# An attention stage re-ordered by a second search, with short operations moved between VectorE, ScalarE and GpSimd

## The chip, the core and the metric

The kernel runs on one core of a Trainium2 chip. The metric is the device time of one execution in microseconds (us); the median of three timed runs stands for a version. The trace names the engines PE (TensorE's matrix multiplications), PEld (its weight loads), DVE (VectorE), ACT (ScalarE), POOL (GpSimd) and SP (SyncE, which issues most DMAs).

## What is computed

A two-step attention feeds a mixture of experts with a greedy assignment of tokens:

```python
def sm_attn(qq, kk, vv):
    s = scale * np.matmul(qq, kk.transpose(0, 1, 3, 2))
    s = s - np.max(s, axis=-1, keepdims=True)
    a = np.exp(s)
    a = a / (np.sum(a, axis=-1, keepdims=True) + 1e-09)
    return np.matmul(a, vv)
p_packed = sm_attn(p, k, v)              # 32 packed rows per head
out = sm_attn(q, p_packed, p_packed)     # 8 batches, 8 heads, 576 tokens, 64 wide
...
logits = x @ w_gate                      # x: 4608 tokens x 512, 8 experts
# tokens go to experts in falling order of logit, at most 576 to an expert
h = np.maximum(x[mask] @ w1[e], 0.0)
out[mask] = h @ w2[e]
```

## The kernel before

The work has three parts. **Attention** goes through 16 groups, each of one batch and four heads. **The router** finds, expert by expert, the threshold that gives each expert its 576 tokens. **The experts** run eight times: gather the tokens, two matrix products in split fp32 (three products for one), scatter.

The attention of one group g is a chain of named steps. DMAs `ld_k`, `ld_q`, `ld_v`; `t_k` and `t_q` turn k and q on VectorE (L353, L354); `s1` on TensorE (L368), `max1` (L380), `exp1`, `rec1` on GpSimd (L391), `tr1` (L400), `a_cp`, `mm_pp` (L416, L418) give the packed rows, `pp_ev` scales them, `pp_t` turns them (L433), `pp_hi` and `pp_lo` (L441) split them in a rounded part and a rest. Then `s2` (L368 again), and the second softmax in a turned layout: `t_s` (L470, L472), `max2` (L476), `sub2` (L481), `exp2` (L485), `sum2` (L491 as one reduction on VectorE, or L497 and L499 as a tree of six additions on GpSimd), `rec2` (L503), `nrm2` (L508), `t_a` (L512), `th` (L516) and `tl` (L521). Five products `x0` to `x4` (L543) follow, whose results `xe0` to `xe4` copy out of PSUM on ScalarE (L553) or on VectorE (L551); `x_st` stores them and `x_lg` adds up the router's logits (`xl0` to `xl4` on VectorE, L566 and L568, for the last two groups).

The order of these steps on each engine is found by a planner, `attention_plan`. It holds a table of steps with engine, length and inputs, and a set of waits for buffers; a list scheduler goes through them in time and takes, on each engine, the ready step with the lowest number in `PRIO` (three columns: groups 0 and 1, groups 2 to 12, groups 13 to 15). `OTHER` names the steps, by group, that go to their second engine, VectorE instead of GpSimd or ScalarE, with the lengths in `on_dve`. Numbers from 44 on stand for halves, since groups 14 and 15 do their second softmax in two halves: 44 and 45 are the halves of group 14, 46 and 47 those of group 15. A step with its group is written sub2.12 below, and with a or b for a half. `early` and `late` are VectorE steps of the router that the planner places too: its constants, and the first look at the logits of all but the last group.

Behind attention, `limit_t` to `limit_c` derive the range of thresholds, `build_a` to `build_v` the values to count, `steps(0, 2)` makes two rounds of counting, `found` draws up the list of expert 0's tokens and starts the loads of its weights by a number `ei` that `expert` computes (L964), and `fl` (L1264) tells whether two rounds were enough. From there to the end the experts follow, in an order that a second planner sets.

Of the kernel before, what the change touches and what calls it, by code (L numbers as in the profile page):

```python
# [15 lines left out]
OP = mybir.AluOpType  # L16
AX = mybir.AxisListType
# [33 lines left out]
    'ld_q': (44.062, 1020.3516, -400.897), 'ld_v': (93.4338, 230.7431, 3.103), 't_k': (-303.2684, 1053.8496, 1263.3541),  # L51
    's1': (-344.5301, 1030.018, 1343.4823), 'max1': (-1141.7006, 595.7444, 1747.411), 'exp1': (1482.9927, 300.9519, 957.0636),
    'rec1': (-364.306, -478.1404, -1528.0943), 'rec1b': (469.6087, -649.4928, 805.8052), 'tr1': (-544.6934, 406.9933, 869.3049),
    'a_cp': (-42.2238, -980.4241, -316.4565), 'mm_pp': (-314.1418, 269.0578, -274.3437), 'pp_ev': (161.5907, -716.4717, 357.7413),
# [128 lines left out]
def attention_plan(fn, on_pool, early, late, groups=16):  # L183
# [3 lines left out]
        ('t_k', 'DVE', 1.46, ['ld_k']), ('s1', 'PE', 1.93, ['t_k']), ('max1', 'DVE', .68, ['s1']),  # L187
        ('exp1', 'ACT', 1.0, ['max1']), ('rec1', 'Pool', .17, ['exp1']), ('rec1b', 'DVE', .08, ['rec1']),
        ('tr1', 'PE', .6, ['exp1']), ('a_cp', 'ACT', .66, ['tr1']), ('mm_pp', 'PE', .9, ['a_cp', 'ld_v']),
        ('pp_ev', 'ACT', 1.28, ['mm_pp', 'rec1b']), ('pp_t', 'DVE', .37, ['pp_ev']), ('t_q', 'DVE', 1.46, ['ld_q']),  # L190
        ('s2', 'PE', 2.12, ['pp_t', 't_q']), ('pp_hi', 'ACT', .41, ['pp_ev']), ('pp_lo', 'Pool', .7, ['pp_hi']),
        ('wg_hi', 'ACT', .31, ['s2', 'pp_hi']), ('wg_lo', 'Pool', .17, ['wg_hi', 'pp_lo']),
        ('t_s', 'DVE', .8, ['s2']), ('max2', 'DVE', .64, ['t_s']), ('sub2', 'Pool', 1.12, ['max2']),
# [1388 lines left out]
```

## Time and profile before

| what | value |
|---|---|
| median of 3 runs | 637.77 us (637.51 to 638.63) |
| profiled execution | 643.15 us, span 641.4 us |
| PE busy | 594.6 us, 93% of the span |
| PEld busy | 496.7 us, 77% |
| DVE busy | 412.9 us, 64% |
| ACT busy | 336.1 us, 52% |
| POOL busy | 368.5 us, 57% |
| mean granted TensorE clock | 0.986 |

The busy shares are means over parts with different limits: attention takes the first 148 us or so, the router's first rounds go to 166 us, and the experts hold the rest. The profiled execution is 5.4 us above the median of the runs.

### The profile page before, as it was taken

What the parts mean: (1) busy time and instruction counts of PE and PEld (TensorE: products, weight loads), DVE (VectorE), ACT (ScalarE), POOL (GpSimd) and SP (SyncE); (2) the same over time, 40 slices, a digit from 0 to 9 for tenths busy, and PEclk for the clock granted to TensorE, in tenths of its full rate; (3) what the DMA queues carried; (4) which work ended last, traced back from release to release, by engine and by line L of the source; (5) the groups of instructions that cost most, each with busy time, mean ns of one, the idle gap of its engine ahead of it and who ended that gap; (6) DMA issues with size and microseconds to landing.
All of it is one profiled execution on the core that took longest, in us unless ns stands there. A gap on an engine that the chain in (4) does not pass through costs nothing. (4 is left out here: it accounts for less than half of the span.)

```text
span 641.4 us, 12439 instructions
## 1 busy us (share of the span) xinstructions
PE 594.6 (93%) x4099; PEld 496.7 (77%) x4101; DVE 412.9 (64%) x1508; ACT 336.1 (52%) x853; POOL 368.5 (57%) x592
## 2 busy tenths in 40 slices
PE   6999899983699999999899999998999999999996
PEld 3678677752388888888788788797888989889984
DVE  7899999997666767657557966964792144162111
ACT  5677777762383774764664565385334235233102
POOL 8378676680570793962954783675447756725003
PEclk9899999997999999999999999999999999999998
DMA  8999996332820634432566365438333864812002
GB/s 274 369 341 309 296 319 198 111 112 75 269 68 6 226 107 150 155 108 76 196 231 155 132 214 116 141 137 245 103 100 107 261 157 144 241 44 75 1 1 78
DMA packets 76953, 103.42 MB, mean 161 GB/s; under 512 B 11792, under 2 KB 57104, under 8 KB 76880
## 3 DMA queue, kind: packets, MB, share of 16 engines
q1 hardware_dynamic: 70464, 83.64, 41.2%
q0 software_dynamic: 5888, 18.88, 8.5%
q8 instruction: 35, 0.57, 0.4%
q14 instruction: 38, 0.31, 0.2%
q10 hardware_dynamic: 528, 0.02, 0.1%
HBM read 77.74 MB, written 24.77 MB: 160 GB/s over the span
## 5 line engine op out<-in xcount | busy, mean ns | idle before, releaser
L1159 DVE SCALAR_TENSOR_TENSOR h<-hp,h 128x288 fp32r<-128x288 f32 (+2 forms) x192 | 59.5, 351 | 116.3 <-ACT h L1154 111.8
L1135 POOL TENSOR_TENSOR w2l<-w2s,w2h 128x256 fp32r<-128x256 f32 x124 | 92.0, 773 | 68.6 <-ACT w2h L1129 68.5
L1135 POOL TENSOR_TENSOR w1l<-w1s,w1h 128x256 fp32r<-128x256 f32 x124 | 91.1, 767 | 58.2 <-ACT w1h L1129 51.6
L1168 PE MATMUL y<-w2h,h 128*128 128x512 f32 x256 | 104.5, 408 | 0.0
L1170 PE MATMUL y<-w2h,h 128*128 128x512 f32 x256 | 101.0, 395 | 0.0
L1169 PE MATMUL y<-w2l,h 128*128 128x512 f32 x256 | 101.0, 395 | 0.0
L1148 PE MATMUL hp<-xh,w1h 128*128 128x288 f32 x512 | 91.5, 301 | 4.6 <-DVE h L1159 1.7
L1148 PE MATMUL hp<-xl,w1h 128*128 128x288 f32 x512 | 90.6, 299 | 0.6 <-DVE xl L1111 0.3
L1154 ACT ACTIVATE h<-hp 128x288 fp32r<-128x288 f32 x128 | 48.7, 406 | 80.4 <-issue 37.4
L1148 PE MATMUL hp<-xh,w1l 128*128 128x288 f32 x512 | 90.4, 298 | 0.0
L1148 PEld LDWEIGHTS hp<-xh,w1h 128*128 128x128 f32 x512 | 77.1, 188 | 10.8 <-DVE h L1159 1.7
L868 ACT ACTIVATE ja<-Vt,nT 128x288 bf16<-128x288 f32 x118 | 63.2, 536 | 36.7 <-DVE nT L894 34.5
L1148 PEld LDWEIGHTS hp<-xl,w1h 128*128 128x128 f32 x512 | 74.9, 188 | 1.3 <-DVE xl L1111 0.5
L1201 POOL DMA_INDIRECT out_dram<-xg,gi x40 | 39.1, 979 | 63.7 <-DVE fl L1427 36.9
L1148 PEld LDWEIGHTS hp<-xh,w1l 128*128 128x128 f32 x512 | 74.6, 188 | 0.1
L1129 ACT CAST w1h<-w1s 128x1024 fp32r<-128x1024 f32 x32 | 33.5, 1047 | 56.2 <-DMA w1s<-in_moe_w_dram 17.8
L1067 POOL DMA_INDIRECT xg<-xd,gi x40 | 39.0, 975 | 32.4 <-DVE Lw L989 21.7
L1170 PEld LDWEIGHTS y<-w2h,h 128*128 128x128 f32 x256 | 48.0, 187 | 11.5
L1169 PEld LDWEIGHTS y<-w2l,h 128*128 128x128 f32 x256 | 48.1, 188 | 8.2
L1168 PEld LDWEIGHTS y<-w2h,h 128*128 128x128 f32 x256 | 48.0, 188 | 8.3
L1129 ACT CAST w2h<-w2s 128x1024 fp32r<-128x1024 f32 x32 | 33.5, 1048 | 32.4 <-issue 13.3
L543 PE MATMUL xp<-P,th 128*128 128x264 f32 (+1 forms) x154 | 37.1, 329 | 7.0 <-ACT xs L553 4.5
(269 smaller groups left out, 1146.1 us busy)
## 6 DMA issues: line engine op xcount, KB each, us to landing
w1s<-in_moe_w_dram SPq DMA_DIRECT2D x32, 512.0 KB, 6.0
w2s<-in_moe_w_dram SPq DMA_DIRECT2D x32, 512.0 KB, 4.3
kl<-in_k_dram SPq DMA_DIRECT2D x16, 576.0 KB, 5.4
ql<-in_q_dram SPq DMA_DIRECT2D x16, 576.0 KB, 6.2
vl<-in_v_dram SPq DMA_DIRECT2D x32, 256.0 KB, 5.2
xd<-xs SPq DMA_DIRECT2D x32, 256.0 KB, 3.3
xg<-xs SPq DMA_DIRECT2D x20, 288.0 KB, 6.3
xs<-xg SPq DMA_DIRECT2D x20, 256.0 KB, 3.8
```

Of the source, the lines that this page charges most:

```text
L543: nc.tensor.matmul(xp[:m, :264], T[a, g][:, o:o + m], T[w, g], start=i == 0, stop=i == 2)
L868: nc.scalar.activation(ja, Vf, AF.Sign, bias=S_['nT'][:, j:j + 1], scale=-1.0, accum_out=cp[:, j:j + 1])
L1067: nc.gpsimd.indirect_dma_start(out=X['xg', k, c][:m], out_offset=None, in_=xd, in_offset=bass.IndirectOffsetOnAxis(ap=X['gi', k][:m, c:c + ...
L1129: nc.scalar.copy(X[n + 'h', k, q], X[n + 's', k, q])
L1135: eng.tensor_sub(X[n + 'l', k, q][r], X[n + 's', k, q][r], X[n + 'h', k, q][r].bitcast(F32))
L1148: nc.tensor.matmul(X['hp', k, f, n], X[W, k, q][:, d, 128 * r:128 * r + 128], X[Z, k][:, d, 288 * n:288 * n + 288], start=i + d == 0, stop ...
L1154: nc.scalar.activation(X['h', k, f][:, 288 * n:288 * n + 288], X['hp', k, f, n], AF.Relu)
L1159: V.scalar_tensor_tensor(h[:, o:o + b - a], p[:, a - 288 * n:b - 288 * n], 0.0, h[:, a:b].bitcast(F32), op0=OP.max, op1=OP.subtract)
L1168: nc.tensor.matmul(y, hh, wh, start=f == 0, stop=False)
L1169: nc.tensor.matmul(y, hh, wl, start=False, stop=False)
L1170: nc.tensor.matmul(y, hl, wh, start=False, stop=f == 7)
L1201: s = nc.gpsimd.indirect_dma_start(out=out, out_offset=bass.IndirectOffsetOnAxis(ap=X['gi', k][:m, t:t + 1], axis=0), in_=X['yo', k, t][:m ...
```

## The change

`PRIO` holds new numbers throughout, and `OTHER` other steps, so that steps of attention change places on all engines and some change their engine. The planner's table gets other lengths (of 29 rows and 6 entries of `on_dve`), `wg_hi` now waits for `t_s`, and two dependences are added. `bf` is taken from the logits directly on the first round, without `best` and an addition. `limit_b`'s product, `expert(0)` and `fl` go from VectorE to GpSimd, `limit_c`'s copy to ScalarE, and the second `build_t` stands ahead of the first `build_v`.

```diff
-    'p_ld_0': (-908.3844, 0.0, 0.0), 'p_t_0': (-275.3561, 0.0, 0.0), 'p_b0_0': (-1206.1704, 0.0, 0.0),
+    'p_ld_0': (-2253.0361, 0.0, 0.0), 'p_t_0': (21.1347, 0.0, 0.0), 'p_b0_0': (-815.0743, 0.0, 0.0),
...
-    'xe2': (0,), 'xe0': (1, 3, 4, 5, 6, 7, 11, 13,), 'xe4': (1, 4, 8, 11,), 'sum2': (2, 3, 5, 9, 10, 11, 13, 44, 45, 46, 47,),
-    'sub2': (3, 11, 12, 13, 44,), 'xe1': (3, 6, 7, 8, 9, 11,), 'pp_lo': (5, 7,), 'nrm2': (5, 11, 45,), 'tl': (6, 44, 45,),
-    'xe3': (8, 11, 15,), 'pp_ev': (14,),}
+    'sum2': (1, 3, 6, 11, 12, 13, 44, 45, 46, 47,), 'xe0': (1, 10, 12,), 'xe4': (1, 2, 6, 8, 9, 15,),
+    'xe1': (3, 6, 8, 10, 12, 13, 14,), 'xe2': (3, 7, 10, 13,), 'nrm2': (4, 44, 46,), 'tl': (6, 8,), 'pp_lo': (7,),
+    'xe3': (9, 11, 13,), 'sub2': (13,),}
...
-    on_dve = {'pp_ev': .72, 'pp_lo': .48, 'sub2': .68, 'sum2': .55, 'nrm2': .8, 'tl': .7}
+    on_dve = {'pp_ev': .76, 'pp_lo': 1.6, 'sub2': 1.1, 'sum2': .64, 'nrm2': .8, 'tl': 1.2}
...
+            P.dep((f'xl{c}', g), (f'xe{c}', g))
+    for g in range(1, groups):
+        P.dep(('x_lg', g - 1), ('x_lg', g))
...
-        V.tensor_scalar(bm[:, :4], C['lim'][:1], bm[:, 4:], None, op0=OP.mult)
+        nc.gpsimd.tensor_scalar(bm[:, :4], C['lim'][:1], bm[:, 4:], None, op0=OP.mult)
...
-        V.tensor_copy(st0, S_['pm'][:, :4])
+        nc.scalar.copy(st0, S_['pm'][:, :4])
...
+    def build_f(a, b):
+        V.reduce_max(bf[:, a:b], L0[:, a:b], axis=AX.X)
...
-    build_a(L0, 31, 36)
+    build_f(31, 36)
+    build_e(L0, 31, 36)
     limit_b()
     build_b(L0, 31, 36)
+    build_t(1, 2)
     build_v(0, 1)
-    build_t(1, 2)
...
-        expert(0)
+        expert(0, nc.gpsimd)
...
-    V.tensor_scalar(fl, mk, 1.0, None, op0=OP.is_ge)
+    nc.gpsimd.tensor_scalar(fl, mk, 1.0, None, op0=OP.is_ge)
```

On VectorE the first large move is in the middle of attention. Before, between `max2.5` and `max1.8`, stand `rec2.4`, `pp_t.6` and the subtraction `pp_lo.5` (L441):

```order
L476 TENSOR_REDUCE mx<-sb 128x18
L503 RECIPROCAL sm<-sm 128x18
L433 STREAM_TRANSPOSE PT<-pf_156 128x4x2x32
L441 TENSOR_TENSOR P_1084<-pf_158,P_1069 128x256
L380 TENSOR_REDUCE st<-s_1056 128x1
```

With the change the same place holds `rec2.4`, `max2.5`, the product `nrm2.4` (L512 is the former L508), `pp_t.6`, `t_a.4` and a copy `xe1.3`:

```order
L507 RECIPROCAL sm<-sm 128x18
L480 TENSOR_REDUCE mx<-sb 128x18
L512 TENSOR_TENSOR e_169<-e_169,sm 128x18x32
L437 STREAM_TRANSPOSE PT<-pf_156 128x4x2x32
L516 STREAM_TRANSPOSE at<-e_169 128x576
L555 COPY xs<-xp 128x264
```

`pp_lo.5` has gone to GpSimd, and `nrm2.4` has come from there.

On GpSimd, before, `pp_lo.10` (L441) is followed by `tl.8` (L521), `sub2.9` (L481), `wg_lo.10`, `sub2.10`, `nrm2.9` (L508), `rec1.13` and `pp_lo.11`, and there is no sum:

```order
L441 TENSOR_TENSOR P_1674<-pf_157,P_1662 128x256
L521 TENSOR_TENSOR tl<-at,th 128x576
L481 TENSOR_TENSOR sb<-sb,mx 128x576
L452 TENSOR_TENSOR P_1674<-wf,P_1662 128x8
L481 TENSOR_TENSOR sb<-sb,mx 128x576
L508 TENSOR_TENSOR e_168<-e_168,sm 128x18x32
L391 TENSOR_SCALAR st<-st 128x1
L441 TENSOR_TENSOR P_1818<-pf_158,P_1811 128x256
```

With the change `pp_lo.10` is followed by `sub2.10`, `nrm2.9`, `wg_lo.10` and the tree of `sum2.10` (L501 and L503); the tree of `sum2.9` stands a few rows ahead:

```order
L445 TENSOR_TENSOR P_1720<-pf_157,P_1701 128x256
L485 TENSOR_TENSOR sb<-sb,mx 128x576
L512 TENSOR_TENSOR e_168<-e_168,sm 128x18x32
L456 TENSOR_TENSOR P_1720<-wf,P_1701 128x8
L501 TENSOR_TENSOR su<-e_169 128x18x16
L501 TENSOR_TENSOR su<-su 128x18x8
L501 TENSOR_TENSOR su<-su 128x18x4
L501 TENSOR_TENSOR su<-su 128x18x2
L501 TENSOR_TENSOR su<-su 128x18
L503 TENSOR_TENSOR sm<-su,e_169 128x18
L395 TENSOR_SCALAR st<-st 128x1
```

`sum2.9` and `sum2.10` were reductions on VectorE; on GpSimd each is six additions in a row. `tl.8` has gone to VectorE.

Behind attention, on VectorE, the flag and the number of the expert stood between the test (L934) and the assignment (L955, L956):

```order
L933 SCALAR_TENSOR_TENSOR key<-pcv,act_79 128x8
L934 TENSOR_REDUCE mk<-key 128x1
L1264 TENSOR_SCALAR fl<-mk 128x1
L964 TENSOR_SCALAR ei<-mk 128x1
L955 SCALAR_TENSOR_TENSOR m_2468<-bf,Tf,kk 128x36
```

With the change they are on GpSimd, behind the last `tl` halves and `limit_b`'s product:

```order
L525 TENSOR_TENSOR tl<-at,th 128x256
L525 TENSOR_TENSOR tl<-at,th 128x320
L817 TENSOR_SCALAR bmax<-lim,bmax 1x4
L1276 TENSOR_SCALAR fl<-mk 128x1
L975 TENSOR_SCALAR ei<-mk 128x1
L1280 TENSOR_LOAD fl
```

On VectorE the assignment now follows the test directly. From the list of expert 0's tokens on, all engines have the same instructions in the same order as before.

## Rows read from the trace of the kernel before

**Rows 1.** Busy time by stretch: us, then busy (and instructions) of each engine, clock, DMA
```profile
43.59:85.97 42.38, 40.25 (x408) 31.49 (x397) 42.22 (x89) 31.88 (x99) 31.27 (x56) 1.00 0.93 297
85.97:121.86 35.89, 35.21 (x334) 27.07 (x332) 34.78 (x80) 26.83 (x83) 24.18 (x40) 1.00 0.67 217
134.92:148.21 13.29, 9.61 (x54) 7.07 (x54) 12.49 (x43) 9.27 (x28) 7.79 (x16) 1.00 0.41 135
176.66:641.40 464.74, 447.50 (x2795) 390.19 (x2795) 255.29 (x1078) 223.76 (x526) 254.16 (x358) 1.00 0.42 130
```

**Rows 2.** Single lines on DVE: count, shortest/median/longest ns, first and last start
```profile
L441 DVE TENSOR_TENSOR P<-pf,P x2: 956/1878/2801, 61.1 to 82.0; 128x256 fp32r<-128x256 f32 x2
L481 DVE TENSOR_TENSOR sb<-sb,mx x5: 702/1278/1455, 46.5 to 133.5; 128x576 f32<-128x576 f32 x4, 128x256 f32<-128x256 f32 x1
L508 DVE TENSOR_TENSOR e<-e,sm x3: 740/759/953, 71.2 to 137.5; 128x576 f32<-128x576 f32 x2, 128x320 f32<-128x320 f32 x1
L521 DVE TENSOR_TENSOR tl<-at,th x3: 422/691/1580, 79.8 to 141.0; 128x576 fp32r<-128x576 f32 x1, 128x256 fp32r<-128x256 f32 x1, 128x320 fp32r<-128x320 f32 x1
L491 DVE TENSOR_REDUCE sm<-e x11: 409/722/772, 45.0 to 139.9; 128x18 f32<-128x594 f32 x7, 128x8 f32<-128x264 f32 x2, 128x10 f32<-128x330 f32 x2
L551 DVE COPY xs<-xp x21: 370/392/435, 40.5 to 138.8; 128x264 f32<-128x264 f32 x17, 64x264 f32<-64x264 f32 x4
L829 DVE TENSOR_TENSOR bf<-best,tkn x8: 164/196/841, 143.6 to 400.9; 128x36 f32<-128x36 f32 x6, 128x31 f32<-128x31 f32 x1, 128x5 f32<-128x5 f32 x1
```

**Rows 3.** Timeline around pp_lo.5: start us, length us, instruction
```profile
61.09 2.80 DVE L441 TENSOR_TENSOR P<-pf,P 128x256 fp32r<-128x256 f32 x1
...
61.29 1.15 POOL L508 TENSOR_TENSOR e<-e,sm 128x576 f32<-128x576 f32 x1
62.40 1.15 POOL L481 TENSOR_TENSOR sb<-sb,mx 128x576 f32<-128x576 f32 x1
```

**Rows 4.** Single lines on POOL, and the first and last addition of one sum tree
```profile
L441 POOL TENSOR_TENSOR P<-pf,P x14: 723/736/1287, 18.9 to 138.7; 128x256 fp32r<-128x256 f32 x14
L481 POOL TENSOR_TENSOR sb<-sb,mx x13: 617/1160/1165, 27.0 to 136.8; 128x576 f32<-128x576 f32 x10, 128x320 f32<-128x320 f32 x2, 128x256 f32<-128x256 f32 x1
L508 POOL TENSOR_TENSOR e<-e,sm x15: 617/1157/1676, 32.7 to 141.2; 128x576 f32<-128x576 f32 x12, 128x256 f32<-128x256 f32 x2, 128x320 f32<-128x320 f32 x1
L521 POOL TENSOR_TENSOR tl<-at,th x15: 730/1417/1730, 36.2 to 143.5; 128x576 fp32r<-128x576 f32 x13, 128x256 fp32r<-128x256 f32 x1, 128x320 fp32r<-128x320 f32 x1
L391 POOL TENSOR_SCALAR st<-st x16: 291/291/310, 13.5 to 118.5; 128x1 f32<-128x1 f32 x16
...
122.85 0.83 POOL L497 TENSOR_TENSOR su<-e 128x288 f32<-128x288 f32 x1
...
125.38 0.25 POOL L499 TENSOR_TENSOR sm<-su,e 128x18 f32<-128x18 f32 x1
```

**Rows 5.** Timeline of TensorE's weight loads, one of each step of a group
```profile
39.05 0.47 PEld L400 LDWEIGHTS tr<-ident,a 128*128 128x128 f32 x4
...
39.59 0.30 PEld L543 LDWEIGHTS xp<-P,th 128*128 128x128 f32 x2
...
39.95 0.31 PEld L543 LDWEIGHTS xp<-P,th 128*128 128x128 f32 x2
...
43.06 0.49 PEld L416 LDWEIGHTS pp<-vl,ah 128*32 128x32 f32 x32 [0.20 <-issue]
...
43.89 1.78 PEld L368 LDWEIGHTS s<-kt,pb 128*128 128x128 f32 x8
...
128.54 4.13 PEld L368 LDWEIGHTS s<-qt,PT 128*128 128x128 f32 x16
```

**Rows 6.** Timeline of DVE behind the test of expert 0
```profile
157.59 0.15 DVE L1264 TENSOR_SCALAR fl<-mk 128x1 int32<-128x1 f32 x1
157.99 0.15 DVE L964 TENSOR_SCALAR ei<-mk 128x1 int32<-128x1 f32 x1 [0.25 <-issue]
158.06 0.25 DVE L955 SCALAR_TENSOR_TENSOR m<-bf,Tf,kk 128x36 f32<-128x36 f32 x1
```

More of the change, by code (lines that the diff above doesn't have):

```diff
@@ L46 @@
 PRIO = {
[4 rows of a table removed]
[L51 to L54, printed above, removed]
@@ L55 @@
-    'pp_t': (407.1754, 606.5689, -1229.8079), 't_q': (695.8205, 825.9429, -370.0736), 's2': (-794.6307, 741.2802, 2398.137),
-    'pp_hi': (-723.6531, 448.1908, 701.421), 'pp_lo': (-429.332, 864.5909, 1010.5893), 'wg_hi': (502.9458, 528.2387, 366.4379),
-    'wg_lo': (-312.3693, 588.8234, -2038.7443), 't_s': (-1154.8118, -1672.1268, -1138.1028), 'max2': (1034.498, 203.305, 465.7759),
[6 rows of a table removed]
-    'x_st': (-873.4582, 764.4405, 433.8428), 'x_lg': (925.5813, 1787.2819, 277.4565), 'xl0': (0.0, 0.0, -402.6867),
@@ L65 @@
-    'xl1': (0.0, 0.0, -303.2386), 'xl2': (0.0, 0.0, 398.5571), 'xl3': (0.0, 0.0, 70.6172), 'xl4': (0.0, 0.0, 1127.0073),
-    'pool': (217.3758, 0.0, 0.0), 'early': (-328.196, -328.196, -328.196),}
[4 rows of a table added]
+    'ld_k': (-1760.2216, -156.7231, 801.3859), 'ld_q': (-218.1023, 2614.5663, -43.3332), 'ld_v': (-65.1975, 1156.2557, -1520.3253),
+    't_k': (485.5666, 1563.9445, 2097.2793), 's1': (-265.7176, 1652.9167, 3517.6274), 'max1': (-909.8639, 1115.2801, 661.5914),
+    'exp1': (2501.6702, 588.4202, 1231.1806), 'rec1': (281.503, -1242.3491, 176.3584), 'rec1b': (842.6925, -4.9454, 1420.201),
@@ new lines @@
+    'tr1': (-679.5092, 968.5393, 1094.0628), 'a_cp': (-210.0346, -784.641, -1014.8614), 'mm_pp': (615.4683, 103.7742, -54.4934),
+    'pp_ev': (-349.3777, -715.5504, 421.6149), 'pp_t': (440.3049, -1131.1555, -3362.1251), 't_q': (1809.0416, 764.8617, -514.5116),
+    's2': (-381.8827, 1210.3272, 2392.5627), 'pp_hi': (-1515.059, 446.4511, 1037.0842), 'pp_lo': (-270.2996, 2190.8834, 599.3373),
+    'wg_hi': (-201.4728, 1442.772, 278.4172), 'wg_lo': (-650.0906, 404.677, -613.0894), 't_s': (-2258.5452, -1278.8686, -1658.3292),
[7 rows of a table added]
@@ L68 @@
+    'x_st': (-2196.2085, 527.5867, 755.5803), 'x_lg': (1601.0665, 1931.2626, 1336.4588), 'xl0': (0.0, 0.0, -784.0472),
+    'xl1': (0.0, 0.0, -2983.1289), 'xl2': (0.0, 0.0, 1177.1917), 'xl3': (0.0, 0.0, -751.9761), 'xl4': (0.0, 0.0, 2564.817),
+    'pool': (358.9113, 0.0, 0.0), 'early': (-1440.0938, -1440.0938, -1440.0938),}
 SPLIT = {14, 15}
 OTHER = {
-    'xe2': (0,), 'xe0': (1, 3, 4, 5, 6, 7, 11, 13,), 'xe4': (1, 4, 8, 11,), 'sum2': (2, 3, 5, 9, 10, 11, 13, 44, 45, 46, 47,),
-    'sub2': (3, 11, 12, 13, 44,), 'xe1': (3, 6, 7, 8, 9, 11,), 'pp_lo': (5, 7,), 'nrm2': (5, 11, 45,), 'tl': (6, 44, 45,),
@@ L186, in attention_plan @@
         ('ld_k', 'DMA', .42, []), ('ld_q', 'DMA', .42, []), ('ld_v', 'DMA', 1.26, []),
[L187 to L193, printed above, removed]
+        ('t_k', 'DVE', 1.4, ['ld_k']), ('s1', 'PE', 1.98, ['t_k']), ('max1', 'DVE', .68, ['s1']),
+        ('exp1', 'ACT', .97, ['max1']), ('rec1', 'Pool', .17, ['exp1']), ('rec1b', 'DVE', .08, ['rec1']),
+        ('tr1', 'PE', .48, ['exp1']), ('a_cp', 'ACT', .66, ['tr1']), ('mm_pp', 'PE', .86, ['a_cp', 'ld_v']),
+        ('pp_ev', 'ACT', 1.28, ['mm_pp', 'rec1b']), ('pp_t', 'DVE', .37, ['pp_ev']), ('t_q', 'DVE', 1.38, ['ld_q']),
+        ('s2', 'PE', 1.95, ['pp_t', 't_q']), ('pp_hi', 'ACT', .41, ['pp_ev']), ('pp_lo', 'Pool', .7, ['pp_hi']),
+        ('wg_hi', 'ACT', .31, ['t_s', 'pp_hi']), ('wg_lo', 'Pool', .17, ['wg_hi', 'pp_lo']),
+        ('t_s', 'DVE', .73, ['s2']), ('max2', 'DVE', .64, ['t_s']), ('sub2', 'Pool', 1.12, ['max2']),
         ('exp2', 'ACT', .6, ['sub2']), ('sum2', 'Pool', 2.71, ['exp2']), ('rec2', 'DVE', .16, ['sum2']),
@@ L829, in build_a, with build_e @@
         V.tensor_add(bf[:, c], best[:, c], tk[:, c])
+        build_e(src, a, b)
+    def build_f(a, b):
+        V.reduce_max(bf[:, a:b], L0[:, a:b], axis=AX.X)
+    def build_e(src, a, b):
+        c = slice(a, b)
         V.tensor_tensor(eq[:, c], src[:, c], bf[:, c, None].to_broadcast([128, b - a, 8]), op=OP.is_ge)
@@ L960, in member, with expert @@
         V.tensor_scalar(S_['mb'], asg, mk, None, op0=OP.is_equal)
-    def expert(n):
+    def expert(n, eng=V):
         X['ei', n] = small([128, 1], "ei", I32)
-        V.tensor_scalar(X['ei', n], mk, -1.0, 8.0, op0=OP.mult, op1=OP.add)
+        eng.tensor_scalar(X['ei', n], mk, -1.0, 8.0, op0=OP.mult, op1=OP.add)
     def check_a():
@@ L1205, in scatter @@
             scat.append(s)
-    before(on_pool, [(4.8, on_dve), (.4, init)], [(.45, lambda: limit(0)), (1.0, lambda: build_a(L0, 0, 31)), (.9, lambda: (build_b(L0, 0, 31), build_s())), (.8, lambda: build_k(0, 31))])
+    before(on_pool, [(4.8, on_dve), (.4, init)], [(.5, lambda: limit(0)), (.42, lambda: build_f(0, 31)), (.44, lambda: build_e(L0, 0, 31)), (.9, lambda: (build_b(L0, 0, 31), build_s())), (.8, lambda: build_k(0, 31))])
     first = ctx.enter_context(ExitStack())
```

19 rows, old and new, of the table PRIO are left out of this document.

## The prediction

> **What bounds the kernel now.** I read the busy time by stretches first [rows 1]. The first four are cut where VectorE starts `t_s` of groups 3, 8 and 13, of the first half of group 15, and where the last logit is added at 148.21 us. The third of them, 13 us long, is not shown. Two things stand there. Between groups 3 and 13 VectorE is busy for 42.22 of 42.38 us and 34.78 of 35.89 us: it is full, at 78.27 us for ten groups or 7.83 us a group. GpSimd has room in the same stretches, 31.27 and 24.18 us, ScalarE too. And in the experts TensorE is busy for 447.5 of 464.7 us; that part is bound by TensorE and has the same instructions in the same order after the change, so I carry its time over whole. What can move is when attention ends, and how long the router needs behind it.
>
> TensorE is the next limit in attention. Its own need for a group comes from its weight loads [rows 5]: `tr1` 0.54 us (39.05 to 39.59), one x 0.36 us (39.59 to 39.95), five of them 1.8 us, `mm_pp` 0.83 us (43.06 to 43.89), `s1` 1.78 us, `s2` 2.07 us (half of 4.13). That makes 7.0 us a group, 90% of the pace of 7.83 us.
>
> **What leaves VectorE in attention, and what comes.** Names are those of the change; the prices come from single lines on VectorE [rows 2].
>
> - `pp_lo.5` leaves. Its row is 2.80 us long, 1.84 us more than the other one of its shape.
> - `sub2` of groups 3, 11 and 12 and the first half of 14 leave, one stays: the shortest, two medians and the longest of the five, 0.70 + 1.28 + 1.28 + 1.46 = 4.7 us.
> - `nrm2` of 5, 11 and the second half of 14 leave (0.74 + 0.76 + 0.95 = 2.45 us). Group 4 and the first halves of 14 and 15 come; a half of 256 columns has no row of its own on VectorE, so I bound it by 0.42 (the shortest `tl`, 320 columns) and 0.95 and take 0.70. That is 2.15 us; net 0.3 us saved.
> - `sum2`: four leave, three come, one reduction of 0.72 us saved.
> - `tl`: group 8 comes, whole. Bounds are 0.70 (the shortest two-input operation of its shape, `sub2`) and 1.58 (the one `tl` of that shape). I take 1.58, the same operation. The two halves of group 14 leave, 0.42 + 0.69. Net 0.5 us added.
> - `xe`: fifteen copies leave, sixteen come, 0.39 us added.
> - `pp_ev.14` leaves; priced as the shortest two-input row, 0.42 us.
> - `build_f` drops two additions, 0.84 us on 31 columns and 0.16 us on 5: 1.0 us.
>
> Sum: 2.80 + 4.7 + 0.3 + 0.72 - 0.5 - 0.39 + 0.42 + 1.0 = 9.05 us. Neighbouring rows on VectorE overlap a little, and about ten fewer instructions run, so I call it **8.5 us**.
>
> The first price needs a word, since it is the largest single item. `pp_lo.5` runs from 61.09 to 63.89 us, and two GpSimd operations of 1.15 us each run inside it, one right behind the other [rows 3]; it ends after both. The Trainium skill ("SBUF — State Buffer", the section on the two separate sides) says that such a VectorE operation and a GpSimd one hold a shared pair of ports by an exclusive lock for a whole instruction. By that rule one GpSimd operation ahead would be the worst, 0.96 + 1.15 = 2.1 us at most, and the sum would be 0.7 us smaller; the row shows two, and I go by the row. The operation that leaves takes its wait along.
>
> **What GpSimd and ScalarE get.** GpSimd takes [rows 4] one sum tree more, 2.78 us (122.85 to 125.63), three whole `sub2` at 1.16 and a half at 0.62, one `pp_lo` at 0.74, one whole `nrm2` at 1.16, about half a microsecond less for the halves of `nrm2`, and for `tl` one of 1.42 us less against two halves of 0.73 and about 0.8: 8.6 us in all. Most of its place is free. It is not free between groups 7 and 10. Before, these four groups hold there 4 `sub2`, 2 trees, 4 `nrm2`, 4 `tl` and 3 `pp_lo`: 4.6 + 5.6 + 4.6 + 5.7 + 2.2 = 22.7 us. After, two trees more and one `tl` less: 26.9 us. `rec1` (0.29 us), `wg_lo` and `x_lg` add about 1 us a group, an estimate: 30.9 us against 31.3 us at the old pace, and against 29.2 us at a pace of 7.3 that VectorE alone would allow. So I take **1.7 us** off for GpSimd. ScalarE gets one `pp_ev` of four activations and loses a copy; it has 10 us free in each 42, and I cost that at nothing. If `pp_ev` came late, `s2.14` would, by about a microsecond.
>
> **The last group.** From 134.92 us to 148.21 us group 15's second softmax goes through four engines [rows 1]. Some 1.8 us of the 8.5 lie here (halves of `tl` and `nrm2`, the two additions, less the copies and `nrm2` halves that come). In a chain with a hop after each step most of that buys nothing; what I leave in is the long addition, 0.5 of its 0.84 us, for it stands ahead of logit copies in VectorE's queue. Against it, GpSimd now has two `tl` halves ahead of group 15's last operations: 0 to 1.5 us, taken as 0 because they wait for nothing that group 15 needs first. So attention ends 8.5 - 1.8 - 1.7 + 0.5 = **5.5 us** earlier.
>
> **Behind attention.** Of the three operations, the product of `limit_b` leaves VectorE for GpSimd, where a 1-column operation takes 0.29 us [rows 4] plus two hand-overs. TensorE's second transposition stands behind the multiplication that waits for it, and both copies of `build_v` now wait for that. What VectorE no longer does is thereby spent: -0.2 to +0.3, taken as 0. The flag and the number at 157.59 and 157.99 us, with 0.25 us of idle time between, stand ahead of the assignment at 158.06 us [rows 6]: 0.45 us off the path to the token list, if the idle time belongs to them. The loads of expert 0's weights wait for the number, which GpSimd makes after the flag, 0.29 + 0.29 us plus a hand-over behind the test, about 0.1 us later than now. Lists gain and weights do not: I take 0.2 us, between 0 and 0.45.
>
> **Sum.** 5.5 + 0.2 = 5.7 us earlier. The terms come from an execution of 643.15 us, which would become 637.5; that execution lies 5.4 us above the median of the runs, and I take the difference over as it is: 637.77 - 5.7 = **632.1 us**.
>
> **Rivals.**
>
> *TensorE keeps its pace.* It needs 7.0 us a group and spends 7.83. If each group keeps half a microsecond or more of the waits it has now (for copies, for `ah`), VectorE becomes idle instead of faster, and only the operations at both ends count: 1.3 to 3.5 us, about 635.3 us. For it: PE busy 35.21 of 35.89 us between groups 8 and 13, and the relief I counted asks for 98% of TensorE there. Against it: a busy PE also counts its own filling, and its weight loads take 27.07 us there.
>
> *Everything counts.* GpSimd absorbs its four heavy groups and the tail gains as well: 8.5 + 0.45 us, 628.8 us. The planner's room of several groups between `tl` and x speaks for it.
>
> *GpSimd becomes the bound, and the kernel slower.* In groups 4 to 12 GpSimd now has 9 `sub2`, 6 trees, 8 `nrm2`, 7 `tl` and 8 `pp_lo`. At the medians, with 1 us of short ones, that is 61 us or 6.8 a group. If the lengthened forms became the rule as VectorE and GpSimd meet more often (1.17, 2.78, 1.68, 1.73 and 1.29 us, the longest of rows 4), it would be 72 us or 8.0 a group, 1.5 us more than the pace of now allows for nine groups, with 1.6 us for the two `tl` halves at the end: about 640.9 us. It decides from 70.5 us on, where GpSimd's groups pass 7.83 us. Against it: the medians are close to the shortest rows, and fewer two-input operations on VectorE mean fewer meetings.
>
> *Nothing comes of it.* The moves only exchange one wait for another, or `ei`'s delay eats the gain: within 1.3 us of 637.8.
>
> **Chances and range.** A measurement of this kernel tells about 0.2% from no change, 1.3 us. My forecast (3.5 to 7 us off) has 0.58, TensorE's pace 0.22, everything 0.08, nothing 0.07, GpSimd 0.05. Faster is thus 0.88, same 0.07, slower 0.05. The range from 629.0 to 636.2 us takes in the forecast, most of TensorE's case and the edge of the full relief, with the unknown prices (`nrm2` halves, `tl.8`, the `tl` halves at the end, some 1.5 us either way); about 0.16 is left out.
>
> **What would show it.** Right: the last logit is added near 142.7 us instead of 148.21, the first count of the router moves as much, VectorE is still full between `t_s.3` and `t_s.13` but needs 74 us or so for it, POOL's busy time in attention is 8 to 9 us higher, and everything from the first expert on is the old profile moved to the left. TensorE's case: VectorE idle for several microseconds, released by PE, in the middle of attention. GpSimd's case: `t_a` and `sum2`'s followers on VectorE and `th` on ScalarE waiting for POOL, in groups 8 to 12. I am wrong if `t_s.15a` starts later than 133 us, or if the stretch from there to the last logit grows by more than 1.5 us.

## The result, and the profile after

The changed kernel takes 630.92 us, the median of 4 runs (629.88 to 632.03), beside 637.96 us for the kernel before (637.51 to 638.63). The ratio is 0.9892, 95% interval 0.9863 to 0.992: 7.0 us or 1.1% faster. The forecast was 632.1 us in a range from 629.0 to 636.2. The sign, the range and the size held. The reason given for it did not, and most of what follows is about that.

The profiled execution of the change took 631.25 us, its span 629.3 us. First its busy time by stretch, cut as [rows 1] were, at the starts of `t_s` of groups 3, 8, 13 and of the first half of group 15, at the last logit (141.58 us) and at the first matmul of the experts. The columns are those of [rows 1].

```profile
43.75:81.97 38.22, 38.22 (x409) 30.43 (x412) 37.00 (x85) 31.47 (x98) 33.71 (x62) 1.00 0.97 322
81.97:120.02 38.05, 38.00 (x404) 29.73 (x393) 34.93 (x82) 29.17 (x91) 32.91 (x58) 1.00 0.68 220
120.02:130.12 10.10, 9.50 (x90) 7.59 (x89) 9.59 (x23) 7.97 (x23) 7.68 (x15) 1.00 0.36 118
130.12:141.58 11.46, 8.85 (x54) 6.76 (x52) 10.73 (x39) 6.84 (x21) 8.79 (x15) 1.00 0.47 155
171.00:629.30 458.30, 447.61 (x2795) 391.16 (x2795) 255.05 (x1078) 223.33 (x526) 252.99 (x358) 1.00 0.42 132
```

The kernel before has this for the stretch that [rows 1] leave out:

```profile
121.86:134.92 13.06, 11.22 (x131) 8.64 (x131) 12.51 (x27) 7.58 (x21) 11.46 (x21) 1.00 0.29 93
```

Three things are to be seen. The ten groups between `t_s.3` and `t_s.13` take 76.27 us instead of 78.27: only 2.0 us of the gain are here. In them TensorE is busy for 76.22 us, without a gap, while VectorE, which was full before, is now idle for 4.3 us (37.00 + 34.93 = 71.93 busy). And the end of attention, from `t_s.13` to the last logit, shrank from 13.06 + 13.29 = 26.35 us to 21.56: 4.8 us. Measured from `t_s.0`, the last logit comes 115.71 us later instead of 123.13, 7.4 us less. From the last logit to the first expert it then takes 29.4 us instead of 28.5, but this stretch differs as much from one execution to the next: 28.9 to 30.0 us in the traces of the change, `old_head`, `mixed_head`, `after_max` and the three kernels with single operations put back (all below), and 29.8 us in `before_max`, which has the router of before. The experts are the old ones; the longer stretch in [rows 1] is that execution's own (another profiled execution with the same experts, under `before_max` below, has 458.85 us).

What VectorE waited for in the two middle stretches (the engine, tile and line that waited, who ended it; us in total, times, longest):

```profile
DVE sm L507 <- POOL sm L503: 1.5, 2, 0.8
DVE sb L474 <- PE s L372: 1.4, 3, 0.7
DVE xs L555 <- PE xp L547: 0.8, 2, 0.6
```

Of these 3.7 us, 2.2 are waits for TensorE. The same view lists nothing for TensorE in these stretches.

### The profile page after: what moved, and what is told of

The parts are those of the page before. It is cut to its first block, busy times and chain, and to the rows that moved or that the text cites. A ratio compares the mean times of both kernels' runs of the same rounds, so it can differ in the third digit from the quotient of the medians.

```text
span 629.3 us, 12447 instructions
## 1 busy us (share of the span) xinstructions
PE 592.8 (94%) x4101; PEld 498.4 (79%) x4101; DVE 402.0 (64%) x1494; ACT 336.4 (53%) x857; POOL 375.8 (60%) x607
## 5 line engine op out<-in xcount | busy, mean ns | idle before, releaser
L896 DVE SCALAR_TENSOR_TENSOR g<-pc,thr,s4r 128x3 f32<-128x3 f32 x66 | 14.4, 218 | 43.2 <-PE pc L891 42.9
```

The costliest lines, as they stand in the source:

```text
L896: V.scalar_tensor_tensor(g, S_['pc'][:, :3], thr, s4[:, i:i + 1].to_broadcast([128, 3]), op0=OP.is_gt, op1=OP.mult, accum_out=S_['ns', i])
```

## The experiments

The prediction's theory: VectorE is full between groups 3 and 13, so what leaves it is time won. The rivals: TensorE holds the pace, or the order does, which decides whether a released microsecond meets work that is ready. All runs are compared by the stretch from `t_s.3` to the last logit, since the beginning differs by up to 2 us from one execution to the next. "TensorE idle" is that stretch less TensorE's busy time.

| kernel | `t_s.3` to `t_s.13` | to the last logit | sum | TensorE idle | VectorE busy |
|---|---|---|---|---|---|
| before | 78.27 | 26.35 | 104.62 | 8.3 | 102.0 |
| the change | 76.27 | 21.56 | 97.83 | 3.3 | 92.3 |
| old_head | 76.26 | 21.57 | 97.83 | | |
| new_head | 78.26 | 27.30 | 105.56 | | |
| before_max | 77.04 | 26.93 | 103.97 | 6.2 | 96.7 |
| after_max | 76.48 | 21.56 | 98.04 | 3.4 | 87.1 |
| before_two | 77.20 | 26.36 | 103.56 | 11.2 | 100.5 |
| after_two | 73.46 | 21.32 | 94.78 | 5.6 | 91.3 |
| order_only | 84.03 | 24.46 | 108.49 | 12.0 | 96.6 |
| engines_only | 85.38 | 26.54 | 111.92 | 11.3 | 94.5 |
| pplo_dve | 77.04 | 21.56 | 98.60 | 3.7 | 93.0 |
| sub2_dve | 77.58 | 21.90 | 99.48 | 4.6 | 94.2 |
| sums_dve | 76.25 | 21.57 | 97.82 | 3.3 | 93.2 |
| mixed_head | 76.27 | 21.54 | 97.81 | | |

TensorE's granted clock is 1.00 all through this stretch in most of these traces. In `new_head`, `before_max`, `before_two`, `after_two` and `order_only` it fell to 1.2 GHz for a part of the end of attention, in `engines_only` for two short parts of the middle. What that costs can be read from `new_head`, which has the attention of before. From `t_s.15a` to the last logit it takes 14.50 us at a mean clock of 0.76, where the kernel before takes 13.29 at 1.00 [rows 1]; `before_max` is disturbed alike:

```profile
135.21:149.71 14.50, 11.48 (x54) 9.29 (x54) 12.93 (x43) 9.40 (x28) 7.77 (x16) 0.76 0.38 123
133.33:147.48 14.15, 11.46 (x54) 9.29 (x54) 12.97 (x43) 9.56 (x28) 7.88 (x16) 0.76 0.39 127
```

So the sums of `new_head`, `before_max`, `before_two` and `after_two` are a microsecond or so too long, an estimate from these rows. Up to `t_s.15a` the clock is full in `before`, `new_head`, `before_max`, `before_two`, the change, `after_max` and `after_two`; from `t_s.3` to there they take 91.33, 91.06, 89.82, 89.97, 86.37, 86.58 and 83.05 us.

### Attention and router apart

`old_head` is the change with the router of before, `new_head` the kernel before with the router of the change (without the split of `build_a`). The edits undo or make these lines, and swap the second `build_t` with the first `build_v`:

```diff
-        nc.gpsimd.tensor_scalar(bm[:, :4], C['lim'][:1], bm[:, 4:], None, op0=OP.mult)
+        V.tensor_scalar(bm[:, :4], C['lim'][:1], bm[:, 4:], None, op0=OP.mult)
-        nc.scalar.copy(st0, S_['pm'][:, :4])
+        V.tensor_copy(st0, S_['pm'][:, :4])
-        expert(0, nc.gpsimd)
+        expert(0)
-    nc.gpsimd.tensor_scalar(fl, mk, 1.0, None, op0=OP.is_ge)
+    V.tensor_scalar(fl, mk, 1.0, None, op0=OP.is_ge)
```

Expected of `old_head`: 

> The changed attention with the router's head of before: limit_b's product, limit_c's copy, the number of expert 0 and the flag are back on VectorE, and build_v(0, 1) stands ahead of the second build_t. Theory (the hand-over to GpSimd and the later transposition cost 0.7 us, the shorter queue of VectorE behind the test gives back 0.3): the first count comes 3.0 to 3.2 us after the last logit instead of 3.76, the kernel is 0.3 to 0.9 us faster than the change, 6 to 8 us below before. Rival (a lower granted TensorE clock between attention and the experts is what costs the 0.7 us): the first count still comes 3.6 us or more after the last logit, and the time is that of the change. Last logit in both: 141.6 us.

Measured: 631.63 us (630.04 to 632.48), ratio 0.9911 [0.988, 0.9941]. The first count comes 3.3 us after the last logit, at the same lower clock as in the change (see the last section), but the kernel is not faster than the change: the theory's 0.3 to 0.9 us are missed.

Expected of `new_head`: 

> The attention of before with the changed operations behind it: limit_b's product, expert 0's number and the flag on GpSimd, limit_c's copy on ScalarE, the second build_t ahead of the first build_v. build_a is left as it was. Theory: the last logit stays at 148.2 us, the first count comes 0.6 to 0.8 us later than before, the assignment 0.3 us earlier against the test; the kernel is between 0.2 us faster and 0.9 us slower than before. Rival (the three operations that leave VectorE carry a good part of the gain): 1 to 2 us faster than before.

Measured: 636.66 us, ratio 0.9976 [0.996, 0.9992]. The theory missed; 1.5 us less lies in the rival's range. Its profiled execution took 644.39 us, far from its median, so its trace can't say where these 1.5 us are.

The attention alone gives most of it: 0.9911 or 5.7 us, beside 0.9892 or 6.9 us, and the intervals overlap. Both comparisons leave the router's edits a gain, 1.2 and 1.5 us. The traces show 0.1 us or less of it up to the assignment, as the section on the reasons shows, so what the rest is stays open.

### Less work on VectorE alone

`after_max` and `before_max` take the first softmax's maximum over 18 of its 576 scores, so `max1` is 0.15 us long instead of 0.73; the rest of the scores is left out of the maximum, and nothing else changes.

```diff
-        nc.vector.reduce_max(st[:, 0:1], T['s1', g].rearrange("p t b y -> p (t b y)"), axis=AX.X, negate=True)
+        nc.vector.reduce_max(st[:, 0:1], T['s1', g][:, 0].rearrange("p b y -> p (b y)"), axis=AX.X, negate=True)
```

Expected of `before_max`: 

> The kernel before, with the same shorter max1. Theory (VectorE was the bound before): the last logit comes 4 to 7 us earlier than 148.2. Rival (waits between engines set the pace before as well, and the new order alone brought the gain): at most 2 us earlier.

Measured: 637.91 us beside 638.0. Its stretches from `t_s.3` to `t_s.8` and on to `t_s.13`:

```profile
43.51:84.14 40.63, 39.18 (x381) 31.03 (x369) 38.86 (x88) 31.42 (x98) 30.16 (x53) 1.00 0.95 302
84.14:120.55 36.41, 35.95 (x367) 27.72 (x370) 32.87 (x80) 27.16 (x84) 25.21 (x42) 1.00 0.68 220
```

VectorE has 5.3 us less to do (38.86 + 32.87 = 71.73 instead of 77.00), about as much as the change takes from it there, and the last logit comes 0.65 us earlier, or 1.6 us beside `new_head`, whose end ran at the same clock of 0.76. Up to `t_s.15a`, at full clock, it is 1.2 to 1.5 us. That is the rival's range; the rest became waiting. This contradicts the prediction's first sentence: a VectorE that is busy for 98% of a stretch was not what set its length.

Expected of `after_max`: 

> The change, with max1 taken over the first 18 of the 576 scores of a row alone (any number near the scores will do as the shift of the exponent), which takes 0.5 to 0.6 us from VectorE in each of 16 groups, some 9 us, in the same order. Theory (with the change TensorE is the bound in the middle of attention, busy 76.2 of 76.3 us between group 3 and group 13): the last logit comes at most 2.5 us earlier than 141.6. Rival (VectorE is still the bound): 4 us or more earlier.

Measured: 630.89 us, as the change. VectorE is busy 5.2 us less (87.1) and the last logit comes 0.2 us later. In the change, a shorter VectorE buys nothing.

### Less work on TensorE alone

`after_two` and `before_two` leave the product of `th` and `P1` out of each x.

```diff
-        for i, (a, w) in enumerate((('th', 'P0'), ('th', 'P1'), ('tl', 'P0'))):
+        for i, (a, w) in enumerate((('th', 'P0'), ('tl', 'P0'))):
-            nc.tensor.matmul(xp[:m, :264], T[a, g][:, o:o + m], T[w, g], start=i == 0, stop=i == 2)
+            nc.tensor.matmul(xp[:m, :264], T[a, g][:, o:o + m], T[w, g], start=i == 0, stop=i == 1)
```

These two and the next two ran on another chip, on which the kernel before takes 645.28 us (19 runs); its experts are longer there (468.5 us in `before_two`). Totals are compared within these four, stretches of attention with all.

Expected of `after_two`: 

> The change, with each x made of two products instead of three: the product of th and P1 is left out, about 0.12 us of TensorE for each of the 80 x, nothing else touched. If TensorE is the bound with the change (busy 76.22 of 76.27 us between t_s.3 and t_s.13): the stretch takes 70 to 72 us, where VectorE's 71.9 busy us stop it, and the last logit comes 4 to 7 us earlier after t_s.3 (91 to 94 us instead of 97.83). If VectorE or the hand-overs bound it: the stretch keeps 75.5 us or more and the last logit moves by less than 2 us.

Measured: the stretch takes 73.46 us and the last logit comes 3.05 us earlier (94.78). Both theories missed: it lies between them. Up to `t_s.15a`, at full clock, the gain is 3.3 us.

```profile
43.02:80.48 37.46, 35.93 (x373) 27.43 (x365) 36.62 (x85) 30.36 (x98) 33.49 (x61) 1.00 0.99 329
80.48:116.48 36.00, 35.18 (x353) 26.41 (x353) 34.62 (x82) 28.75 (x91) 32.62 (x58) 1.00 0.69 230
```

TensorE now has gaps (71.11 of 73.46 us busy) and VectorE is close behind (71.24). In the change TensorE is the first limit, with 3 us to VectorE and the hand-overs.

Expected of `before_two`: 

> The same cut in the kernel before: each x without the product of th and P1. If VectorE alone is the bound before (77.0 busy us of 78.27 between t_s.3 and t_s.13): the stretch keeps 77 us or more and the last logit comes less than 1.5 us earlier after t_s.3 (104.62 us). If TensorE is the bound there too: the stretch takes 73 to 75 us and the last logit comes 4 us or more earlier. If both engines hold it by turns, 1.5 to 4 us.

Measured: 1.06 us earlier (103.56), and the ten groups take 77.20 us. TensorE's idle time rises from 8.3 to 11.2 us. By its numbers this is the first case named ahead, VectorE alone, which `before_max` rules out; the end ran at a mean clock of 0.80, and up to `t_s.15a`, at full clock, 1.1 to 1.4 us are won. So in the order of before neither a shorter VectorE nor a shorter TensorE, by 4 to 5 us in the ten groups, moves `t_s.15a` by more than 1.5 us.

### The order and the engines apart

The change's attention consists of an order of issue and a table of engines. `order_only` keeps the change's order and puts every operation of attention back on the engine it had before; `engines_only` keeps the order of before and takes the change's engines.

```diff
-    attention_plan(fn, on_pool, early, late).emit()
+    plan = attention_plan(fn, on_pool, early, late)
+    OTHER.clear()
+    OTHER.update(...)
+    plan.emit()
```

Expected of `order_only`: 

> The change's order with the engines of before: every operation is issued in the change's order, but each one that the change moved between VectorE and GpSimd or ScalarE goes back to the engine it had before, inside attention; the head is the change's. Theory 1 (VectorE's relief makes the gain): VectorE gets back about 6 us of work between t_s.3 and t_s.13 and is full there; that stretch takes 78 us or more (76.27 with the change, 78.27 before), from t_s.3 to the last logit about 103 us (97.83 with the change, 104.62 before), the whole 635 to 637 us. Theory 2 (the order makes the gain, TensorE's work being ready when its turn comes): the stretch stays within 1 us of 76.27 or the tail pays for it, from t_s.3 to the last logit 98 to 100 us, the whole 631 to 633 us.

Measured: 650.33 us, ratio 1.0059 [1.0022, 1.0096], slower than before, where both theories expected a gain. In the trace the stretch is 108.49 us, 3.9 us longer than before. But the traced execution took 656.48 us, 6 us above the median, and in the stretch ScalarE waits twice for a DMA, as in no other of these traces:

```profile
92.37 0.38 ACT L557 COPY xs<-xp 128x264 f32<-128x264 f32 x1 [1.56 <-DMA xd<-xs]
99.93 0.75 ACT L557 COPY xs<-xp 128x264 f32<-128x264 f32 x2 [1.56 <-DMA vl<-in_v_dram]
```

So the loss is shown by the ratio, and its size in the stretch is not.

Expected of `engines_only`: 

> The other half alone: the order of before, each operation of attention on the engine that the change gives it; the head is that of before. Theory 1 (VectorE's relief): VectorE has about 6 us less between t_s.3 and t_s.13, so the stretch takes 73 to 75 us, from t_s.3 to the last logit 98 to 101 us, the whole 632 to 635 us. Theory 2 (the order): as with the short maximum in the order of before, the freed time turns into waits; t_s.3 to the last logit 103 to 106 us, the whole 637 to 640 us.

Measured: 652.88 us, ratio 1.0094 [1.0052, 1.0136]; the stretch is 111.92 us, 7.3 us longer than before. For 6.8 us of it TensorE ran at 1.2 GHz, so up to 3.4 of the 7.3 us can be the clock's.

Neither theory expected this. Each half alone loses, 0.6% and 0.9% of the whole, and both together gain 1.1%. VectorE has 5.4 and 7.5 us less to do in them than before, and TensorE's idle time is 12.0 and 11.3 us all the same. In `order_only` no operation of attention has left VectorE: its five `sub2`, two `pp_lo`, three `nrm2` and three `tl` are the same as before and take 8.9 us together instead of 14.6, by the new order alone. How moving an operation to a free engine costs time is seen in `engines_only`, in the timeline of four engines from 108 us on (start, length, engine, line, operation, and in brackets the idle time before it and what ended it). The sums of groups 9 and 10, single reductions of about 0.72 us on VectorE before, are now two trees on GpSimd, one right behind the other (L497):

```profile
108.42 0.82 POOL L497 TENSOR_TENSOR su<-e 128x288 f32<-128x288 f32 x1
...
111.16 0.81 POOL L497 TENSOR_TENSOR su<-e 128x288 f32<-128x288 f32 x1
...
113.85 1.16 POOL L508 TENSOR_TENSOR e<-e,sm 128x576 f32<-128x576 f32 x1
115.04 0.78 DVE L512 STREAM_TRANSPOSE at<-e 128x576 f32<-128x576 f32 x1 [2.84 <-POOL e L508]
...
117.60 0.69 DVE L476 TENSOR_REDUCE mx<-sb 128x18 f32<-128x576 f32 x1
118.37 1.16 POOL L481 TENSOR_TENSOR sb<-sb,mx 128x576 f32<-128x576 f32 x1 [0.34 <-DVE mx L476]
119.56 0.68 ACT L485 ACTIVATE e<-sb 128x576 f32<-128x576 f32 x1 [2.27 <-POOL sb L481]
...
121.26 0.54 PE L368 MATMUL s<-qt,PT 128*128 128x320 f32 x1 [2.08 <-ACT a L387]
```

VectorE's next operation, `t_a` (L512), waits 2.84 us for the product `nrm2` (L508) behind the trees, and all that stands behind it on VectorE waits along, `max2` of group 11 (L476) too. So `sub2` of group 11 is late, ScalarE waits 2.27 us for it, another group's `exp1` (L386, L387) stands behind that in ScalarE's queue, and TensorE waits 2.08 us for the place that `exp1` frees. The trees are on GpSimd in the change too, but in its order VectorE waits for GpSimd for 1.7 us in all ten groups; here it is 10.4 us (5.5 for sums, 4.9 for `nrm2`).

### Single operations put back

In the change's order, single operations go back to VectorE: `pp_lo` of group 5; `sub2` of groups 3, 11, 12 and the first half of 14; the sums of groups 9 and 10. The edit is one line, for the first:

```diff
+    OTHER['pp_lo'] += (5,)
```

Expected of `pplo_dve`: 

> The change with one operation put back: pp_lo of group 5 on VectorE, at its place in the change's order. Theory 1 (the prediction's price): t_s.3 to t_s.8 takes 1.8 to 2.8 us more than with the change (38.22 us), and the last logit comes as much later after t_s.3 (97.83 us). Theory 2 (a joint plan with room): VectorE has 1.2 us of idle time in that stretch and the meeting with GpSimd is another one, so the operation is 0.4 to 1 us long there and the stretch keeps 38.2 to 38.7 us.

Measured: `t_s.3` to `t_s.8` 38.92 us, 0.7 more, the last logit 0.77 us later; 632.54 us. On VectorE and GpSimd, in the timeline:

```profile
63.54 1.16 POOL L485 TENSOR_TENSOR sb<-sb,mx 128x576 f32<-128x576 f32 x1
...
64.08 0.89 DVE L445 TENSOR_TENSOR P<-pf,P 128x256 fp32r<-128x256 f32 x1
```

The operation that took 2.80 us before [rows 3] takes 0.89 us here: theory 2, with the stretch a little above its range.

Expected of `sub2_dve`: 

> The change with the largest term of the prediction put back: sub2 of groups 3, 11, 12 and of the first half of 14 on VectorE, at their places in the change's order; in the sum they stand with 4.7 us. Theory 1 (each operation costs what its row lasts on the full VectorE): from t_s.3 to the last logit 101 to 103 us (97.83 with the change). Theory 2 (TensorE bounds the change's order, VectorE has 4.3 us of idle time between t_s.3 and t_s.13): less than 2 us more, 98 to 99.8 us. Theory 3 (a chain of softmax that comes late at one group is not caught up): more than 5 us, and TensorE waits for tl or th several times.

Measured: the last logit 1.65 us later (99.48), 636.19 us in one run. The four operations as they came back (the first half of 14 is the last row):

```profile
51.07 0.72 DVE L485 TENSOR_TENSOR sb<-sb,mx 128x576 f32<-128x576 f32 x1
111.76 0.71 DVE L485 TENSOR_TENSOR sb<-sb,mx 128x576 f32<-128x576 f32 x1
115.84 0.74 DVE L485 TENSOR_TENSOR sb<-sb,mx 128x576 f32<-128x576 f32 x1
...
128.51 0.42 DVE L485 TENSOR_TENSOR sb<-sb,mx 128x256 f32<-128x256 f32 x1
```

2.59 us in all instead of the 4.7 us of the sum. Theory 2 holds: they cost less than they last. The whole of this one run is 5 us longer than the profiled run of the change; the other 3 us lie ahead of `t_s.3` and behind the last logit.

Expected of `sums_dve`: 

> The change with the sums of groups 9 and 10 (sum2) back on VectorE, at their places in the change's order; GpSimd gets 5.5 us less between t_s.8 and t_s.13, VectorE 1.5 us more. The prediction's deduction of 1.7 us (GpSimd is overloaded in groups 7 to 10): the stretch from t_s.8 to t_s.13 becomes 0.8 to 2 us shorter than the 38.05 us of the change. If TensorE (38.00 us busy in it) bounds the stretch: within 0.4 us of 38.05. If the order has no room for VectorE's 1.5 us there: 0.5 to 1.5 us longer.

Measured: `t_s.8` to `t_s.13` 37.90 us instead of 38.05, the last logit where it was, 631.54 us.

```profile
82.57:120.47 37.90, 37.85 (x395) 29.62 (x385) 35.88 (x83) 29.25 (x91) 28.34 (x46) 1.00 0.67 218
```

GpSimd has 4.6 us less to do there (28.34 instead of 32.91), and it buys 0.15 us. TensorE holds the stretch.

### A router between the two

`mixed_head` is `old_head` with the flag left on GpSimd.

```diff
-    V.tensor_scalar(fl, mk, 1.0, None, op0=OP.is_ge)
+    nc.gpsimd.tensor_scalar(fl, mk, 1.0, None, op0=OP.is_ge)
```

Expected: 

> The change's attention and the router as before, except that the flag stays on GpSimd; limit_b, limit_c and the number of expert 0 are on VectorE, and build_v stands where it stood before. If the late copies of build_v cost the 0.4 us that the change's trace seems to show between the last logit and the first count, and the flag on GpSimd saves 0.27 us: from the last logit to the assignment 9.7 to 9.9 us (10.28 with the change, 9.85 before), and the whole is 0 to 0.6 us below the change. If the router's differences are within the noise: the same total as the change, within 0.2%.

Measured: 631.74 us (630.74 to 632.66), ratio 0.9913 [0.9891, 0.9935]; from the last logit to the assignment 10.03 us, not the 9.7 to 9.9 of the first case. Between the three routers on the change's attention (0.9892, 0.9911, 0.9913) the measurement doesn't tell. No version beat the change.

## Why the prediction was right or wrong

**"VectorE is full", and what leaves it is time won: wrong.** This step carried the sum. VectorE's relief came out as counted in its total, 9.05 us by the rows and 102.00 - 92.25 = 9.75 us measured between `t_s.3` and the last logit, and this was luck: 5.4 of the 9.75 us are there in `order_only` too, where every operation of attention is on its old engine, so only 4.3 us came with the moves that the sum was made of. And relief was not time. In the order of before a relief of 5.3 us gave 0.65 to 1.6 (`before_max`), a relief of 7.5 us by the change's own engine table gave a loss of up to 7.3 (`engines_only`), and in the change another 5.2 us gave nothing (`after_max`). Before, neither VectorE alone nor TensorE alone bound attention. That several engines held it by turns, each through its fixed queue, fits this and is argued: GpSimd and ScalarE were not made shorter, nor two engines at once. TensorE then stood idle for 8.3 us of the 104.62. What the new order and the new table do together is to close 5.1 of these 8.3 us; TensorE's busy time falls by another 1.7 us (96.29 to 94.58) with weight loads of 74.3 and 74.5 us (one `mm_pp` more falls into the stretch of the change), so its work did not shrink and ran closer together.

**TensorE needs 7.0 us a group: too small.** It needs 7.63, for it has no gap in the change's ten groups. The prediction took x at 0.36 us, from two x in a row, and `s1` at 1.78 [rows 5]. In the mixed sequence that the engine really runs, the rows are longer (TensorE in the change, one group's worth of steps):

```profile
100.15 2.14 PE L372 MATMUL s<-kt,pb 128*128 128x288 f32 x8
102.22 0.65 PE L420 MATMUL pp<-vl,ah 128*32 128x64 f32 x32
102.80 0.32 PE L422 MATMUL pp<-vr,ah 64*32 64x64 f32 x8
103.05 0.51 PE L547 MATMUL xp<-P,th 128*128 128x264 f32 x2
...
103.52 0.40 PE L547 MATMUL xp<-P,th 128*128 128x264 f32 x2
...
103.88 2.35 PE L372 MATMUL s<-qt,PT 128*128 128x320 f32 x8
105.82 0.66 PE L547 MATMUL xp<-P,th 128*128 128x264 f32 x2
...
106.44 0.40 PE L547 MATMUL xp<-P,th 128*128 128x264 f32 x2
...
106.81 0.60 PE L404 MATMUL tr<-ident,a 128*128 128x128 f32 x4
...
107.27 0.48 PE L547 MATMUL xp<-P,th 128*64 128x264 f32 x2
...
107.71 2.35 PE L372 MATMUL s<-qt,PT 128*128 128x320 f32 x8
```

From start to start `s1` takes 2.07 us, `mm_pp` 0.83, the x 0.47, 0.36, 0.62, 0.37 and 0.44, `s2` 1.94, `tr1` 0.46: 7.56 us. An x behind another step costs 0.08 to 0.26 us more than one behind an x. With 7.6 instead of 7.0 the prediction's own arithmetic would have left 78.27 - 76 = 2 us in the middle, as measured, and not the 5 us that it put there.

So **"TensorE keeps its pace"**, the first rival, was right on the middle, including its sign (VectorE idle for several microseconds, released by TensorE). It was wrong on the total, 635.3, for it let only the operations at both ends count, 1.3 to 3.5 us.

**The last group: the term was mis-sized.** The prediction took 1.8 us of the relief out and put 0.5 back, because a chain with hops doesn't turn relief into time. From `t_s.13` to the last logit 4.8 us were won. 3.0 of them lie before `t_s.15a`, in the 13 us for which the prediction had no term of its own. TensorE's rows of before in it:

```profile
128.66 4.54 PE L368 MATMUL s<-qt,PT 128*128 128x320 f32 x16
...
135.77 0.51 PE L543 MATMUL xp<-P,th 128*128 128x264 f32 x2 [1.85 <-ACT xs L553]
```

and of the change:

```profile
121.84 2.35 PE L372 MATMUL s<-qt,PT 128*128 128x320 f32 x8
...
127.74 2.35 PE L372 MATMUL s<-qt,PT 128*128 128x320 f32 x8
```

Before, `s2` of groups 14 and 15 ran back to back (16 matmuls), both halves of the second softmax piled up behind them, and TensorE then waited 1.85 us for a copy. In the change they stand 6 us apart, with x and `mm_pp` between. Two more x (147 matmul records instead of 141) are done before `t_s.13`, in a shorter time. That it is this and not the shorter chain of group 15 is read from the two traces and was not tried alone.

**The total came near by luck.** The errors nearly cancel. Attention was to end 5.5 us earlier, 5.0 in the middle and 0.5 at the end; measured from `t_s.0` it ended 7.4 us earlier, 2.0 in the middle, 4.8 at the end and 0.6 ahead of `t_s.3`. Between the last logit and the first expert the trace of the change is 1.0 us longer than that of before, where a gain of 0.2 was forecast; as said above, executions differ by as much there. That is why 632.1 came so near.

**GpSimd gets 8.6 us: right**, 8.4 measured (74.69 to 83.09); the terms listed for it add up to 8.4 as well. **The 1.7 us taken off for its overload in groups 7 to 10: wrong.** The stretch from `t_s.8` is longer than before (38.05 instead of 35.89 us), which looks like it, but `sums_dve` takes the load away and gains 0.15 us. The stretch ahead of it is 4.2 us shorter, and TensorE is full in both. The rival "GpSimd becomes the bound" falls with it.

**`pp_lo.5` at 2.80 us and four `sub2` at 4.7: right, or nearly (the four rows that left add up to 4.4), for the order of before, but no price of the operation.** In the change's order they take 0.89 and 2.59 us, and they lengthen attention by 0.77 and 1.65 us.

**Behind attention, 0.2 us: not won in the traces, and within what can be told.** The idle time ahead of the assignment did not belong to the flag and the number:

```profile
151.46 0.16 DVE L945 TENSOR_REDUCE mk<-key 128x1 f32<-128x9 f32 x1
151.86 0.26 DVE L966 SCALAR_TENSOR_TENSOR m<-bf,Tf,kk 128x36 f32<-128x36 f32 x1 [0.24 <-issue]
```

They are gone, and 0.24 us of "issue" still stand there: the assignment starts 0.24 us behind the end of the test (151.62 us), 0.51 us before (157.55 to 158.06 us, [rows 6]). On the other side the first count of the router starts 3.76 us after the last logit (3.04 before, 3.3 in `old_head`): the transposition behind `limit_b`'s product and the copies behind it are late, as feared, and the "0" for this was 0.4 us too good. To the assignment it is 10.28 us instead of 9.85 before and 10.14 in `old_head`. Some 0.3 us of the change's and of `old_head`'s time is a lower clock: `pplo_dve`, with the router of the change at full clock, takes 3.44 and 9.94 us, and `new_head`, at full clock too, 9.81. So up to the assignment the router's edits lie between a loss of 0.1 us and a gain of 0.05. What the 1.5 us of `new_head` come from stays open.

**The signs named ahead.** The last logit near 142.7 us: 141.58, in an execution that began attention 0.8 us later. POOL 8 to 9 us busier: yes. `t_s.15a` not after 133 us: 130.12. VectorE full, with 74 us for ten groups: no, and this was the sign of the mechanism.

## What to carry to other kernels

That an engine is busy for 98% of a stretch with a fixed order doesn't make it the bound. Make one of its operations short, in the old order, and see whether the end moves; do the same for the next engine; here 4 to 5 us less on either moved it by 1.5 us at most. An order and its table of engines are one plan: a half of a good plan can be worse than the old one, so a moved operation is costed with the queue that waits for it. Price the second engine's need from the mixed sequence that it runs, not from its best repeats, for it is the floor under every relief.
